# GpSimd's sums in pieces of 256 columns and a new order of all operations, in a causal attention with a squared-ReLU feed-forward behind it

## The chip, the cores and the metric

The kernel runs on one core of a Trainium2 chip. A core has a tensor engine (TensorE, PE in the profile, its weight loads PEld), a vector engine (VectorE, DVE), a scalar engine (ScalarE, ACT), GpSimd (POOL) and a sync engine (SP). Each takes its own instructions in the order of the program and waits by semaphores for the others. Transfers between the chip's memory and the core's are issued by SP, ACT or POOL and carried by 16 DMA engines. The metric is the device time of one execution in microseconds; smaller is better.

## The reference

Eight batches of eight heads, 576 tokens, 16 beacon tokens ahead of the keys, head size 64; then a feed-forward layer over all 4608 tokens. Inputs and outputs are float32.

```python
k_all = np.concatenate([beacon_k, k], axis=2)
v_all = np.concatenate([beacon_v, v], axis=2)
scores = scale * np.matmul(q, k_all.transpose(0, 1, 3, 2))
scores = np.where(causal, -1000000000.0, scores)
a = np.exp(scores - scores.max(-1, keepdims=True))
a /= a.sum(-1, keepdims=True) + 1e-09
x = np.matmul(a, v_all)            # then as (4608, 512)
h = x @ w_in                       # 512 -> 2048
r = np.maximum(h, 0.0)
out = (r * r) @ w_out              # 2048 -> 512
```

## The kernel before

**Attention** works on 32 pairs of heads, four pairs a batch; pair p belongs to batch p // 4. The operations have names. `qk*` are the score products (five visits a batch into PSUM strips), `exp*` the exponentials on ScalarE, `mask*` the causal masks on the diagonal blocks of the probabilities `pt` (DVE by a minimum with the constant `tri`, L780; or GpSimd by a select, L776; five a pair), `av{p}.0.{h}` the products with V of one head (15 matmuls, L802), `norm*` the division by the row sum on DVE (L819, L821). From batch 2 on, q, k and v are loaded by GpSimd's queue (`ld{b}q*`, `ld{b}k*`, `ld{b}v*`; L408, L417, with the beacon rows L416 in part 0), q and k are turned by a DMA transpose on SP (`tr*`), and from batch 3 on the result is turned into `xT` by DMA transposes `xt{b}.{t}` (L853). Batches 0 and 1 are turned by TensorE. Batch 0's first rows come by loads on SP and ACT (`fldk*`, `fldq*`), the rest of it by GpSimd (`sld0k1.*`, `sld0q1.*`, L472).

**Feed-forward** works on nine chunks of 512 tokens. `s1.*` is the first layer, `s2.*` the second. In chunks 3 to 8 the first layer, and in chunks 1 to 8 the second, is done by a scheme of seven products of half size instead of eight: blocks of the inputs, of the weights and of the squared activations are first added or subtracted (`xsum{j}.{n}` L961, `asum*` L928, `wsum*` L913, `sum{j}.{n}.{i}` L1163), and the products' results are put together when they leave PSUM (`h*`, L1023 and L1016; `ev*`, L1217). `s2.{j}.{n}.{t}` is product n of chunk j for token half t, eight matmuls; `s1.{j}.{u}.{n}` product n of unit u, four or eight matmuls. Product 6 of the second layer reads sum 2, product 5 sum 1, product 7 sum 3, product 3 sum 4. `sum{j}.{n}.{i}` covers half i of the eight row blocks: 128 x 1024 elements; each may run on DVE or GpSimd. `relu*` and `sq*` are the activations.

**The order** of all operations is written out by hand in the string `SEQUENCE` (L18 on); a letter behind `@` names the engine where there is a choice (`A` ScalarE, `D` DVE, `P` GpSimd). `Order.run` issues the operations in that order, so the string fixes the queue of each engine, the rotation of PSUM banks and strips, and the order of the loads on each DMA queue. An operation's place in the string is not its time: an engine that is ahead runs its part early. 60 filler matmuls (`fill*`, L354) keep TensorE busy while the first data come. The durations in the calls of `add` are figures that are not used at run time.

Of the kernel before, what the change touches and what calls it, by code (L numbers as in the profile page):

```python
# [12 lines left out]
ALU = mybir.AluOpType  # L13
# [4 lines left out]
ones fill19 fillg19 fill7 fillg7 fill47 fill59 fillg59 fillg47 fill10 fill55 fill34 fillg55 fillg34 fill48 fillg48  # L18
fill23 fillg23 fill45 fillg45 fill43 fill2 fillg2 fill25 fillg25 fillg43 fill35 fill27 fillg27 fillg35 fill33 fill32
fillg33 fillg32 fill57 fillg57 fill58 fill22 fill42 fillg58 fillg22 fillg42 fill40 fill11 fillg11 fillg40 fill56  # L20
fillg10 fill36 fillg36 fillg56 fill46 fillg46 fill39 fill31 fillg31 fldk0 ident fldk1 bkl0 fck1 fck0 bkc0 tp0.0.0k
fillg39 ek0.0.0@D fill29 fillg29 fill9 fillg9 fill49 fillg49 fill21 fillg21 tpg0.0.0k fill28 fill51 fillg51 fillg28
tpb0 fill8 fillg8 ekb0 sld0k1.0 tri fldq0 fldq1 ld0v1 sld0q1.0 ld0v0 fldq2 fcq1 fcq0 tp0.0.0q fill26 fillg26 eq0.0.0@A
fill17 fillg17 tpg0.0.0q tp0.0.1k fill52 fillg52 tp0.0.1q fill38 fillg38 ek0.0.1@D eq0.0.1@A tp0.1.0k tp0.1.1k
ek0.1.0@A ek0.1.1@D fcq2@D tpg0.0.1k tpg0.0.1q tpg0.1.1k fldk2 fck3 fcq3@A qk0.0.0 qk1.0.0 fill41 fillg41 tpg0.1.0k
tp0.0.3q fill6 fill54 fillg6 fillg54 fill18 fillg18 tp0.0.3k fill14 fill5 eq0.0.3@D tpg0.0.3q fillg14 fillg5 tp0.1.0q
tp0.1.1q tp0.0.2q exp0.0.0 exp1.0.0 eq0.1.0@A ek0.0.3@D eq0.0.2@A qk3.0.0 qk0.1.0 mask0.0.0@D eq0.1.1@D fck2
mask1.0.0@D tpg0.0.2q tpg0.1.0q tpg0.0.3k fill13 tpg0.1.1q fillg13 fill4 av0.0.0 fillg4 bkl1 exp3.0.0 fill44 fill12
tp0.0.2k qk1.1.0 fillg12 fillg44 sld0k1.2 sld0q1.2 ld0v3 ld0v2 win0 ld0v4 mask3.0.0@P win2 exp0.1.0 fill0 fill30
norm0.0.0 av1.0.0 ek0.0.2@D fillg30 tpg0.0.2k fillg0 norm1.0.0 exp1.1.0 qk1.1.2 av3.0.0 tp0.1.2k xtp0.0.0 xte0.0.0@D  # L30
norm3.0.0 qk2.0.0 exp1.1.2 exp2.0.0 ek0.1.2@D fill1 tp0.1.2q qk0.1.2 mask2.0.0@D eq0.1.2@D fillg1 fill53 fill37
fillg37 fillg53 tpg0.1.2k qk0.1.1 fill16 fillg16 fill3 fillg3 av2.0.0 fill50 fill24 fillg24 tpg0.1.2q exp0.1.2
exp0.1.1 qk1.1.1 fillg50 win1 mask1.1.1@P norm2.0.0 xtp0.0.3 tp0.1.3k xte0.0.3@D qk2.1.1 ek0.1.3@D exp1.1.1
mask0.1.1@P win3 sld1k0.0 sld1q0.0 sld1k0.2 mask1.1.0@D xtp0.0.2 fill15 fillg15 tpg0.1.3k tp0.1.3q fill20 fillg20
eq0.1.3@D xtp0.0.1 mask0.1.0@D qk2.1.0 bkc1 xte0.0.2@D exp2.1.1 exp2.1.0 mask2.1.0@P ld2q6 av1.1.0 norm1.1.0
mask2.1.1@D qk2.1.2 qk3.1.0 tpg0.1.3q xte0.0.1@A av0.1.0 s1.0.3.0 xtp0.1.1 s1.0.8.0 exp2.1.2 exp3.1.0 wout1 sld1q0.2
ld2q7 ld1v1 ld1v0 wout0 ld2q4 zero2 wout2 ld1v3 qk3.1.1 qk3.1.2 norm0.1.0 relu0.8.0@A tpb1 xte0.1.1@D mask3.1.1@D
# [190 lines left out]
def kernel(  # L228
# [709 lines left out]
    def add_first_both(j, G, sq):  # L938
# [18 lines left out]
        for n, o, a, c in ((1, pieces(s[1]), b12, b11), (2, pieces(s[2]), b22, pieces(s[1])), (3, b12, b22, b12),  # L957
                           (4, pieces(s[4]), b21, pieces(s[2]))):
            def emit_x(e, o=o, a=a, c=c):
                for x, y, z in zip(o, a, c):  # L960
                    (nc.vector if e == "DVE" else nc.gpsimd).tensor_tensor(out=x, in0=y, in1=z, op=ALU.subtract)  # L961
# [381 lines left out]
```

## Time and profile before

| what | before |
|---|---|
| median of 3 runs | 324.85 us (324.58 to 325.82) |
| the profiled execution | 325.59 us, span 323.9 us |
| TensorE busy | 313.9 us, 97% of the span, 3882 matmuls |
| VectorE busy | 252.1 us, 78% |
| ScalarE busy | 213.1 us, 66% |
| GpSimd busy | 195.8 us, 60%, 268 instructions |
| granted TensorE clock | 0.999 |
| sums of L1163 on GpSimd | 19, 2.1 to 2.5 us each |

How to read the rows below: L12 is line 12 of the kernel. Rows of groups give line, engine, operation, out<-in by the program's names, shape and count, then busy us and mean ns of one, then the idle time of that engine just before them and what ended it. Rows of a timeline give start and length in us from the span's start, engine, line, operation and count; in brackets the idle time before and who ended it. A row of the waits reads: who waited, on which line, for whom: us in total, times, longest. Matmuls overlap one another, so a row's length can exceed the spacing of matmuls.

### The profile page before, as it was taken

To read this page: it belongs to the slowest core of one execution; us is meant where nothing else is said; L and a number is where in the kernel's file an instruction comes from. 1 tells how busy PE (TensorE), PEld (TensorE's weight loads), DVE (VectorE), ACT (ScalarE), POOL (GpSimd) and SP (SyncE) were. 2 spreads that over 40 slices of the span, in tenths; PEclk is the share of its full clock that TensorE was granted. 3 is DMA by queue.
4 is the path that set the end of the run, shared out by engine and by line. 5 is a ranking of instruction groups with operands and counts; after the bars stand their busy time and mean duration, and the time that the engine had idled before them with its cause. 6 is when DMAs were issued, how large, how long until landed. Compare 5 with 4: busy or idle time off the path is not lost.

```text
span 323.9 us, 9406 instructions
## 1 busy us (share of the span) xinstructions
PE 313.9 (97%) x3882; PEld 247.4 (76%) x3882; DVE 252.1 (78%) x529; ACT 213.1 (66%) x313; POOL 195.8 (60%) x268
## 2 busy tenths in 40 slices
PE   7899999999999999998999999999999989999995
PEld 5569765644886468887788888888898878888884
DVE  2687698758976798789997998896867987695773
ACT  2785588257677794768657996889767545555720
POOL 8574679496189588888293759956606051535340
PEclk9999999999999999999999999999999999999999
DMA  8999999999999999999799969944523430110043
GB/s 162 178 179 200 189 182 114 146 199 178 146 78 157 198 174 84 124 222 155 61 130 135 212 68 128 149 88 142 49 16 91 110 52 0 68 65 2 0 148 113
DMA packets 153188, 39.60 MB, mean 122 GB/s; under 512 B 140730, under 2 KB 148794, under 8 KB 153146
## 3 DMA queue, kind: packets, MB, share of 16 engines
q0 software_dynamic: 103744, 18.10, 71.7%
q1 hardware_dynamic: 48253, 20.29, 30.3%
q10 hardware_dynamic: 1149, 0.62, 0.7%
q8 instruction: 30, 0.49, 0.6%
q14 instruction: 12, 0.10, 0.1%
HBM read 37.22 MB, written 9.44 MB: 144 GB/s over the span
## 4 chain that ended last, share of the span: by engine, by line
PE 89%; DVE 3%; DMA 3%; ACT 2%; issue 1%; POOL 0%; DVEq 0%; POOLq 0%; ACTq 0%
PE ps L1194 28%; PE ps L985 21%; PE ps L1088 13%; PE ps L802 9%; PE strip L649 6%; PE ps L1137 4%; DMA qk_area<-in_k_dram 3%; PE ps L649 2%; PE strip L1194 2%; DVE g L1023 1%; PE ps L870 1%; PE ps L354 1%; ACT pt L747 1%; PE ps L489 1%; PE ps L487 1%
## 5 line engine op out<-in xcount | busy, mean ns | idle before, releaser
L1194 PEld LDWEIGHTS <-g 128*128 128x128 bf16 x768 | 72.7, 98 | 10.8 <-issue 1.4
L747 ACT ACTIVATE pt<-strip 128x1024 bf16<-128x1024 f32 x70 | 70.2, 1032 | 5.7 <-PE strip L649 5.7
L1023 DVE CUSTOM_DVE_ANT_0 g<-ps,spare 128x512 bf16<-128x512 f32 x72 | 48.8, 686 | 17.9 <-PE ps L985 12.1
L1194 PE MATMUL ps<-w_out,g 128*128 128x256 bf16 x480 | 60.9, 273 | 0.0
L776 POOL TENSOR_SCALAR_AFFINE_SELECT pt<-pt 128x256 bf16<-128x256 bf16 (+1 forms) x80 | 33.3, 437 | 27.9 <-ACT pt L747 23.9
L372 ACT COPY spare<-ps 128x512 f32<-128x512 f32 x54 | 31.5, 588 | 25.9 <-PE ps L985 21.7
L1163 POOL TENSOR_TENSOR g<-g 128x1024 bf16<-128x1024 bf16 x13 | 28.0, 2158 | 31.5 <-DVE g L1163 10.8
L408 POOL DMA_DIRECT2D qk_area<-in_q_dram x48 | 35.2, 742 | 17.3 <-DMA qT<-qk_area 14.3
L985 PEld LDWEIGHTS <-w_in 128*128 128x128 bf16 x480 | 39.3, 96 | 7.6 <-issue 2.7
L1088 PE MATMUL ps<-xT,w_in 128*128 128x512 bf16 (+2 forms) x256 | 44.1, 326 | 0.0
L985 PE MATMUL ps<-xT,w_in 128*128 128x256 bf16 (+4 forms) x384 | 42.7, 247 | 0.3 <-DMA xT<-xn 0.2
L802 PE MATMUL ps<-vb,pt 128*128 128x65 bf16 (+1 forms) x960 | 38.5, 194 | 1.8 <-DVE g L1023 0.9
L802 PEld LDWEIGHTS <-pt 128*128 128x128 bf16 (+1 forms) x960 | 35.6, 97 | 5.9 <-issue 2.6
L417 POOL DMA_DIRECT2D vb<-in_v_dram x40 | 34.4, 860 | 6.2 <-DMA qk_area<-in_q_dram 2.3
L1088 PEld LDWEIGHTS <-w_in 128*128 128x128 bf16 x256 | 24.0, 98 | 16.3 <-issue 1.0
L1049 ACT ACTIVATE g<-g 128x1024 bf16<-128x1024 bf16 x31 | 32.2, 1058 | 5.6 <-DVE g L1023 4.1
L821 DVE TENSOR_TENSOR xn<-ps,rcp 128x320 bf16<-128x320 f32 (+2 forms) x64 | 31.5, 492 | 2.2
L985 PEld LDWEIGHTS <-qk_area 128*128 128x128 bf16 x320 | 27.8, 97 | 5.2 <-issue 0.8
L747 ACT ACTIVATE pt<-ps 128x512 bf16<-128x512 f32 x42 | 23.6, 598 | 9.6 <-PE ps L649 8.8
L1194 PE MATMUL ps<-w_sum,g 128*128 128x256 bf16 x224 | 28.9, 273 | 0.0
L985 PE MATMUL ps<-spare,qk_area 128*128 128x256 bf16 x192 | 27.9, 272 | 0.5 <-DVE spare L961 0.5
L649 PEld LDWEIGHTS <-kT 64*128 64x128 bf16 x618 | 19.8, 94 | 10.7 <-issue 7.8
(87 smaller groups left out, 492.0 us busy)
## 6 DMA issues: line engine op xcount, KB each, us to landing
out_dram<-osb SPq DMA_DIRECT2D x16, 512.0 KB, 3.8
qk_area<-in_q_dram POOLq DMA_DIRECT2D x48, 72.0 KB, 4.8
vb<-in_v_dram POOLq DMA_DIRECT2D x24, 128.0 KB, 6.0
qk_area<-in_k_dram POOLq DMA_DIRECT2D x18, 128.0 KB, 4.7
w_in<-in_moe_w_in_dram POOLq DMA_DIRECT2D x4, 512.0 KB, 9.4
w_out<-in_moe_w_out_dram POOLq DMA_DIRECT2D x4, 512.0 KB, 9.2
vb<-in_v_dram POOLq DMA_DIRECT2D x8, 112.0 KB, 5.2
qk_area<-in_k_dram POOLq DMA_DIRECT2D x6, 112.0 KB, 4.5
```

What stands on the lines that cost most here:

```text
L372: nc.scalar.copy(dst, src)
L408: return [nc.gpsimd.dma_start(out=qb[:, g, :, D * u:D * u + D], in_=t[b, c].rearrange("(n p) d -> p n d", p=NP))]
L417: insts.append(nc.gpsimd.dma_start(out=dst[lo:rows], in_=t[b, :, t0:t0 + rows - lo, :].transpose([1, 0, 2])))
L649: nc.tensor.matmul(out, kc[b % 2][hp, c, pr] if b >= NPE else kT[b % 2][hp, pr, 128 * c:128 * c + 128], rhs, start=True, stop=True)
L747: nc.scalar.activation(out, in_, AF.Exp, bias=0.0, scale=scale)
L776: nc.gpsimd.affine_select(out=d[:, :, i], in_=d[:, :, i], compare_op=ALU.is_ge, fill=0.0, base=Nb if m0 + i == 0 else 0, pattern=[[0, 2], ...
L802: nc.tensor.matmul(a[:, at + (t - tl[0]) * (D + 1):at + (t - tl[0] + 1) * (D + 1)], P[0:rr, hj, o:o + 128], vb[b % 2][0:rr, c, 2 * pr + hj ...
L985: nc.tensor.matmul(o[:, i * HT + at:i * HT + at + w], lhs[:, m, f * 128:(f + 1) * 128], part[:, m], start=fresh and i == 0 and at == 0 and ...
L1023: nc.vector._custom_dve(TENSOR_ADD_SAT, out=dst, in0=bank_of(chain), in1=held[keep[added].held[1]].rearrange("p (f t) -> p f t", f=2), s0= ...
L1049: nc.scalar.activation(both, both, AF.Square, bias=0.0, scale=1.0)
L1088: nc.tensor.matmul(h[:, lo - spans[0][0]:hi - spans[0][0]], w_in_sb[:, mc, ft * 128:(ft + 1) * 128], xT[:, mc, lo % RING:lo % RING + hi - lo],
L1194: nc.tensor.matmul(o, lhs[:, f, t * 128:(t + 1) * 128], rhs[:, f], start=fresh and f == 0, stop=f == HF - 1, skip_group_check=True)
```

## The change

Two helpers change. A sum of the activations (`add_sum`) and a sum of the inputs (`emit_x`) stay one instruction on DVE; on GpSimd a sum becomes four instructions of 256 columns (one per row block), and an input sum one instruction per row block and part of the ring, 256 columns or fewer each, where it was one instruction with both row blocks.

```diff
             def emit_x(e, o=o, a=a, c=c):
                 for x, y, z in zip(o, a, c):
-                    (nc.vector if e == "DVE" else nc.gpsimd).tensor_tensor(out=x, in0=y, in1=z, op=ALU.subtract)
+                    if e == "DVE":
+                        nc.vector.tensor_tensor(out=x, in0=y, in1=z, op=ALU.subtract)
+                        continue
+                    for m in range(HM):
+                        nc.gpsimd.tensor_tensor(out=x[:, m], in0=y[:, m], in1=z[:, m], op=ALU.subtract)
...
         def add_sum(n, o, a, c, op, i, deps):
             fs = slice(4 * i, 4 * i + 4)
-            sums[n].append(add(f"sum{j}.{n}.{i}", ("DVE", "POOL"), {"DVE": 0.67, "POOL": 2.12}, lambda e: (nc.vector if e == "DVE" else nc.gpsimd).tensor_tensor(
-                out=o[:, fs], in0=a[:, fs], in1=c[:, fs], op=op), deps=deps))
+
+            def emit(e):
+                if e == "DVE":
+                    nc.vector.tensor_tensor(out=o[:, fs], in0=a[:, fs], in1=c[:, fs], op=op)
+                    return
+                for f in range(4 * i, 4 * i + 4):
+                    nc.gpsimd.tensor_tensor(out=o[:, f], in0=a[:, f], in1=c[:, f], op=op)
+
+            sums[n].append(add(f"sum{j}.{n}.{i}", ("DVE", "POOL"), {"DVE": 0.67, "POOL": 2.12}, emit, deps=deps))
```

The string `SEQUENCE` is replaced as a whole, with the same 1737 words (other letters on some). Counted over the string: sums on GpSimd 19 before, 17 after (45 and 47 on DVE); input sums on GpSimd 6 and 3; masks on GpSimd 78 and 77; evacuations `ev*` on ScalarE 23 and 28, on DVE, where there is a choice, 17 and 12. From chunk 3 on TensorE's own order is nearly the old one; ahead of it it differs much, as do the other engines' orders throughout. Excerpts that are spoken of below, the loads and masks of GpSimd at the end of batch 4 first:

```diff
-... mask18.0.1.1@P mask19.0.0.0@P mask19.0.0.1@P mask18.0.2@P ld6q4 mask18.0.0.1@P ld6q5 ld6q6 mask18.0.1.0@P ld6q2 ld5v2 qk20.2 av18.0.0 sq3.2.1@D norm18.0.0 s1.3.3.3 h3.3.c12 av19.0.0 av18.0.1 av19.0.1 s2.3.2.0 sq3.3.0@A norm18.0.1 norm19.0.1 sum3.1.0@P ...
+... mask18.0.1.1@P ld5v4 ld6q1 mask18.0.1.0@P mask18.0.2@P ld5v3 ld6q2 mask19.0.0.1@P ld6q0 ld6q6 av18.0.0 s1.3.3.4 h3.3.c21@A sq3.3.1@A qk20.2 av18.0.1 s1.3.3.3 norm18.0.0 mask19.0.2@P mask19.0.0.0@P mask19.0.1.0@P mask19.0.1.1@P ld6k4 ld6q7 av19.0.0 sum3.1.0@D sum3.3.0@P ...
```

The start of chunk 7:

```diff
-... av31.0.1 norm31.0.0 h6.3.c22 h6.3.c21@A sq6.3.1@A sq6.2.0@A av30.0.1 norm31.0.1 norm30.0.1 s1.6.3.3 s1.6.3.2 s2.6.2.0 s2.6.2.1 st11 xt6.3 xt6.4 st10 xt6.2 xt7.0 h6.3.c12 h6.3.c11 sq6.3.0@D sum6.1.1@D xsum7.1@D xsum7.2@D s2.6.1.0 s1.7.0.1 s1.7.1.1 h7.0.c1@A s1.7.0.6 h7.0.u2@A s2.6.1.1 sum6.3.1@D xsum7.3@D xsum7.4@D s1.7.0.7 h7.0.u3@A s1.7.0.4 ...
+... av31.0.1 h6.3.c22 h6.3.c21@A sq6.3.1@A norm31.0.0 s1.6.3.3 s1.6.3.2 norm31.0.1 s2.6.2.0 s2.6.2.1 xt6.3 st11 xt7.0 st10 h6.3.c12 h6.3.c11 sq6.3.0@D sum6.1.1@D xsum7.1@D xsum7.2@D xsum7.3@D sum6.3.1@D xsum7.4@D s1.7.0.1 s2.6.1.0 h7.0.c1@A s1.7.0.6 h7.0.u2@A s2.6.1.1 s1.7.0.7 s1.7.1.1 h7.0.u3@A ev6.c1.None@A s1.7.0.4 ...
```

The first operations of the queues at the start (SP; ACT; GpSimd; before, then after):

```diff
-fldk0 fldk1 bkl0 fldk2; fldq0 fldq1 fldq2 fcq1 fcq0; ident sld0k1.0 tri ld0v1 sld0q1.0 ld0v0
+fldk2 fldk1 bkl0 fldk0; fldq0 fldq1 fldq2 fcq0 fcq1; ident tri sld0k1.0 sld0q1.0 ld0v1 ld0v0
```

GpSimd's queue ahead of `av24.0.0` after the change, from the first mask of pair 25, and the second layer of chunk 7 after it:

```diff
+mask25.0.0.1@P ld7q1 ld7v3 ld7k0 ld7k4 ld7k1 ld7v4 ld7q0 ld7k3 ld6v0 ld7q6 ld7q2 ld7v1 mask24.0.0.0@P
...
+s2.7.1.1 s1.8.0.3 sum7.3.1@D sum7.2.1@D h8.0.c12 s2.7.2.0 s1.8.1.6 h8.1.u2@D s1.8.1.2 s2.7.2.1 h8.1.c11 ev7.c1.None@A ev7.c11.None sq8.0.1@A sum7.1.0@P sum7.3.0@P sum7.2.0@P sum7.4.0@P s1.8.1.7 s1.8.2.1 h8.1.u3@D h8.2.c1@A s2.7.6.0
```

More of the change, by code (lines that the diff above doesn't have):

```diff
@@ L17 @@
 SEQUENCE = """
[L18 to L37, printed above, removed]
@@ L98 @@
-mask18.0.0.1@P ld6q5 ld6q6 mask18.0.1.0@P ld6q2 ld5v2 qk20.2 av18.0.0 sq3.2.1@D norm18.0.0 s1.3.3.3 h3.3.c12 av19.0.0
-av18.0.1 av19.0.1 s2.3.2.0 sq3.3.0@A norm18.0.1 norm19.0.1 sum3.1.0@P s2.3.1.0 sum3.1.1@D s2.3.5.0 s2.3.1.1 norm19.0.0
-sum3.3.1@D exp20.2.0.0.0 exp20.2.1.0.0 sum3.3.0@D sum3.2.0@D sum3.2.1@D xt4.2 xt4.1 xt4.0 ev3.c1.None@A s2.3.5.1
-s2.3.2.1 ld5v3 sum3.4.0@P ld6v0 ld6k3 ld6k0 s2.3.6.0 s2.3.6.1 ev3.u2.None@A ev3.c11.None mask20.0.0.0@D mask20.0.0.1@D
-qk20.5 exp20.5.-1.0.0 exp20.5.0.0.0 exp20.5.-1.1.0 s2.3.7.0 s1.4.0.1 s2.3.7.1 h4.0.c1@A ev3.u3.None@A s1.4.0.2 ld6k4
@@ L163 @@
-sum8.3.0@P h8.3.c12 ev7.c12.None sq8.3.0@A s2.8.1.0 s2.8.1.1 sum8.1.1@D sum8.3.1@D sum8.2.0@D sum8.2.1@D s2.8.5.0
-s2.8.2.1 sum8.4.1@P sum8.4.0@D st14 ev7.c21.None@A ev8.c1.0@A s2.8.6.0 ev8.u2.0@D st15 ev8.c1.1@A ev8.c11.None
-st8.0.0.0 s2.8.5.1 s2.8.7.0 ev8.u3.0@D ev8.c22.0 s2.8.6.1 ev8.u2.1@D s2.8.4.0 ev8.c21.0@D st8.1.0.0 st8.0.1.0 s2.8.7.1
-ev8.u3.1@D ev8.c22.1 s2.8.3.0 s2.8.4.1 s2.8.3.1 ev8.c12.0 st8.0.0.256 ev8.c21.1@A ev8.c12.1 st8.1.1.0 st8.0.1.256
+ones fill23 fillg23 fill54 fill58 fillg58 fillg54 fill12 fill15 fill53 fillg53 fillg15 fill7 fillg7 ident tri fill29
@@ new lines @@
+fillg12 fill57 fill22 fillg22 fill43 fillg43 fillg57 fill33 fillg29 fill16 fill40 fillg40 fillg16 fill13 fillg13 fill6
+fill35 fillg35 fill49 fillg49 fillg6 fill21 fillg21 fillg33 fill2 fill39 fillg39 fldq0 fillg2 fill38 fillg38 fill25
+fill20 fillg20 fill59 fillg59 fillg25 fill34 fill44 fillg34 fill37 fillg37 fill41 fill50 fillg41 fillg44 fill48
+fillg50 fill10 fillg10 fillg48 fldk2 fldk1 bkl0 fill32 fill8 fillg32 fillg8 fck3 bkc0 tpb0 fill9 fillg9 fill26 fillg26
+fldq1 fldk0 fldq2 fck1 ekb0 fck0 tp0.0.1k fill19 fillg19 fill3 fillg3 fill46 fillg46 fill1 fillg1 fill42 fillg42
@@ new lines @@
+exp18.11.1.0.0 h3.2.c1@D s1.3.2.6 norm17.0.0 s1.3.3.2 s1.3.3.6 sq3.0.0@D h3.3.c11 h3.2.c11 h3.2.u2@A qk19.13 s1.3.2.7
+sq3.1.0@A h3.2.u3@A av17.0.1 s1.3.2.5 exp19.13.1.0.0 h3.3.u2@D norm17.0.1 s1.3.2.4 h3.2.c21@A h3.2.c22 sq3.1.1@D
+sq3.2.1@D s1.3.3.7 h3.3.u3@A s1.3.3.5 s1.3.2.3 h3.2.c12 h3.3.c22 exp19.13.0.0.0 ld6q3 ld6q4 ld6q5 mask18.0.1.1@P ld5v4
+ld6q1 mask18.0.1.0@P mask18.0.2@P ld5v3 ld6q2 mask19.0.0.1@P ld6q0 ld6q6 av18.0.0 s1.3.3.4 h3.3.c21@A sq3.3.1@A qk20.2
+av18.0.1 s1.3.3.3 norm18.0.0 mask19.0.2@P mask19.0.0.0@P mask19.0.1.0@P mask19.0.1.1@P ld6k4 ld6q7 av19.0.0 sum3.1.0@D
@@ new lines @@
+sum3.3.0@P h3.3.c12 s2.3.2.0 av19.0.1 sq3.2.0@A s2.3.2.1 norm18.0.1 norm19.0.0 norm19.0.1 xt4.2 xt4.0 xt4.1 sq3.3.0@A
+s2.3.1.0 s2.3.1.1 ev3.c1.None@A exp20.2.1.0.0 exp20.2.0.0.0 sum3.1.1@D sum3.3.1@D sum3.2.1@D sum3.2.0@D s2.3.5.0
+s2.3.5.1 s2.3.6.0 s2.3.6.1 sum3.4.0@D ev3.c11.None qk20.5 ev3.u2.None@A exp20.5.-1.1.0 xsum4.1@D xsum4.2@D
+exp20.5.-1.0.0 exp20.5.1.0.0 mask20.0.1.0@D s2.3.7.0 s1.4.0.1 s2.3.7.1 h4.0.c1@A s1.4.0.2 s1.4.0.6 ev3.u3.None@A
+s2.3.4.0 xsum4.4@D mask20.0.2@D h4.0.c11 ev3.c22.None xsum4.3@D s1.4.0.5 s2.3.4.1 h4.0.u2@A exp20.5.0.0.0 s1.4.0.7
@@ new lines @@
+h5.1.c1@D ev4.u2.None@A s1.5.0.5 s1.5.0.7 s2.4.7.0 s1.5.1.6 mask24.0.0.1@D h5.0.u3@A s1.5.0.4 h5.0.c21@A h5.0.c22
+s1.5.0.3 sum4.4.0@D h5.0.c12 h5.1.u2@A s2.4.7.1 qk25.8 s1.5.1.7 ev4.u3.None@D exp25.8.-1.1.0 exp25.8.-1.0.0 s2.4.4.0
+exp25.8.0.0.0 exp25.8.1.0.0 s1.5.1.2 s2.4.4.1 qk27.13 s1.5.1.5 ev4.c21.None@A s1.5.2.1 exp27.13.0.0.0 ld7k4 ld7k1
+ld7v4 ld7q0 ld7k3 ld6v0 mask24.0.1.0@D ld7q6 ld7q2 sq5.0.1@D h5.1.u3@D sum4.4.1@D ld7v1 h5.1.c11 mask24.0.1.1@D
+mask24.0.0.0@P ld7k2 mask27.0.1.0@P mask25.0.2@P ld7v2 mask25.0.1.1@D mask26.0.0.0@P mask24.0.2@D h5.1.c22 av24.0.0
```

249 lines of the change are left out of this document (129 added, 120 removed).

## The prediction

> **What bounds the kernel now.** I read the page's first part and its chain, then who TensorE waits for, then the stretches in which it waits.
>
> ```profile
> span 323.9 us, 9406 instructions
> PE 313.9 (97%) x3882; PEld 247.4 (76%) x3882; DVE 252.1 (78%) x529; ACT 213.1 (66%) x313; POOL 195.8 (60%) x268
> PE 89%; DVE 3%; DMA 3%; ACT 2%; issue 1%; POOL 0%; DVEq 0%; POOLq 0%; ACTq 0%
> ```
>
> TensorE is 97% busy and carries 89% of the chain that ended last; GpSimd carries 0% of it. The change leaves every matmul as it is, so it can only take away or add waits of TensorE. This is all the waiting there is (us in total, times, longest):
>
> ```profile
> PE ps L354 <- DVE ones L348: 1.8, 1, 1.8
> PE ps L487 <- DMA qk_area<-in_k_dram: 1.2, 1, 1.2
> PE ps L802 <- DVE g L1023: 0.9, 1, 0.9
> PE ps L985 <- ACT spare L372: 0.7, 1, 0.7
> PE ps L802 <- DVE pt L780: 0.5, 1, 0.5
> PE ps L985 <- DVE spare L961: 0.5, 1, 0.5
> PE ps L802 <- DVE xn L821: 0.3, 1, 0.3
> PE ps L985 <- DMA xT<-xn: 0.2, 1, 0.2
> ```
>
> The sum is 6.1 us, of which 3.0 (the first two rows) lie in the start, before there is data. The other 3.1 lie in two places: at 153 to 157 us, where the last two pairs of batch 4 are multiplied with V (L802: 0.9 + 0.5 + 0.3), and at 258 to 263 us, where chunk 7 begins (L985: 0.7 + 0.5 + 0.2). Nothing that touches the second half can gain more than 3.1 us, 1.0% of the span.
>
> **The change, part by part.** The profiled execution took 325.59 us for a span of 323.9, so 1.7 us lie around the span; it is 0.74 above the median of 324.85. All terms below are differences, made on the span of 323.9 and then set on the median.
>
> *1. Four pieces for one sum.* One line groups instructions by form (count, then busy us, mean ns); the timeline rows give start and length, for both instructions where it says x2.
>
> ```profile
> L1163 POOL TENSOR_TENSOR g<-g 128x1024 bf16<-128x1024 bf16 x13 | 28.0, 2158 | 31.5 <-DVE g L1163 10.8 <-PE ps L1194 9.7 <-ACT pt L747 8.8
> 224.09 1.30 POOL L961 TENSOR_TENSOR spare<-xT,spare 128x384 bf16<-128x384 bf16 x2 [1.04 <-DVE spare L961]
> 225.36 1.41 POOL L961 TENSOR_TENSOR xT<-xT 128x384 bf16<-128x384 bf16 x2
> ```
>
> Two stretches of the chain give what one product of the second layer (L1194) and two of the first (L985) take on TensorE, 0.87 and 2 x 0.44 us:
>
> ```profile
> 200.16 0.87 PE ps L1194 x8
> 201.03 0.89 PE ps L985 x8
> ```
>
> No sum in 256-column pieces is in this trace. The nearest are those of L961 that cross the ring's end: 512 columns in two pieces (384 and 128) take 1.30 or 1.41 us, so four pieces of 256 take 2.60 to 2.82 against 2.16 for one instruction: 0.44 to 0.66 more each. Below, pieces that cost nothing extra give 0; a gain is excluded, since the columns are the same. I take 0.44, as those pieces run back to back as the new ones will. The new order gives GpSimd 17 sums instead of 19 and 3 input sums (xsum) instead of 6, so its work grows by 17 x 0.44 = 7.5 us and falls by two sums, 4.3 us, and the xsums. It is 60% busy, and no TensorE wait names it: I put it at 0. Its tightest consumer in the new order is sum 2 of chunk 7 (`sum7.2.0@P`): between `s2.7.1.1`, which it must wait for, and `s2.7.6.0`, which reads it, stand five first-layer products and two of the second (5 x 0.44 + 2 x 0.87 = 3.9 us). 2.60 fits, with 1.3 us to spare; one instruction would have left 1.8.
>
> The Trainium skill, GPSIMD Engine Reference, section 2.1, has the cost of one more instruction as one indirect call, some tens of cycles: three more would then cost, as an estimate from that page, about 0.1 us, not 0.44, and the sum stays 0.
>
> *2. What a long sum holds up.* DVE's mask on L780 normally takes 0.28 us (three take 0.64 in a row at 187.78). Beside GpSimd's sums:
>
> ```profile
> 187.78 0.64 DVE L780 TENSOR_TENSOR pt<-pt,tri 128x256 bf16<-128x256 bf16 x3
> 151.01 2.06 DVE L780 TENSOR_TENSOR pt<-pt,tri 128x256 bf16<-128x256 bf16 x2
> 153.21 2.15 POOL L1163 TENSOR_TENSOR s_sum<-g 128x1024 bf16<-128x1024 bf16 x1
> 153.72 0.61 PE L802 MATMUL ps<-vb,pt 128*128 128x65 bf16 x15 [0.87 <-DVE g L1023]
> 154.19 1.33 DVE L780 TENSOR_TENSOR pt<-pt,tri 128x256 bf16<-128x256 bf16 x1
> 155.58 0.94 PE L802 MATMUL ps<-vb,pt 128*128 128x65 bf16 x25 [0.48 <-DVE pt L780]
> ```
>
> The mask at 154.19 ends 0.16 us after the sum at 153.21 does (155.36): it stood still for about 1.05 us. TensorE's 0.48 at 155.58 and the 0.3 on `xn` behind it come from that; no other wait in the list ends on a mask. A piece of 256 columns would hold a mask for 0.65 at most (2.60 / 4). But the largest wait, 0.87, comes from DVE being stuck at 151.01, before any sum starts: GpSimd runs masks and issues loads there. The split doesn't touch that.
>
> *3. The new order at that place.* `sum3.1.0` goes to DVE, and the masks of pair 19 all go to GpSimd, behind masks of 18 and loads. What lies between the end of pair 18's exponentials and `av19.0.0` on its queue: six 128-row masks, two 80-row masks, four q loads, two v loads.
>
> ```profile
> L776 POOL TENSOR_SCALAR_AFFINE_SELECT pt<-pt 128x256 bf16<-128x256 bf16 x69 | 30.2, 454 | 23.0 <-ACT pt L747 19.2 <-ACT pt L671 3.7
> L776 POOL TENSOR_SCALAR_AFFINE_SELECT pt<-pt 80x160 bf16<-80x160 bf16 x11 | 3.6, 333 | 4.8 <-ACT pt L747 4.7
> L408 POOL DMA_DIRECT2D qk_area<-in_q_dram x48 | 35.2, 742 | 17.3 <-DMA qT<-qk_area 14.3 <-DMA w_out<-in_moe_w_out_dram 1.8 <-PE ps L1088 1.2
> L417 POOL DMA_DIRECT2D vb<-in_v_dram x40 | 34.4, 860 | 6.2 <-DMA qk_area<-in_q_dram 2.3 <-DMA qk_area<-in_k_dram 1.6 <-DMA w_in<-in_moe_w_in_dram 1.5
> 146.90 1.84 POOL L776 TENSOR_SCALAR_AFFINE_SELECT pt<-pt 128x256 bf16<-128x256 bf16 x4 [2.33 <-ACT pt L747]
> ```
>
> 6 x 0.454 + 2 x 0.333 + 4 x 0.742 + 2 x 0.860 = 8.1 us from 146.9, when the exponentials free GpSimd: 155.0. TensorE would reach `av19.0.0` at about 154.4 (without the 0.87 at 153.9, and 0.5 of products now stand ahead of it). So 0.6 of waiting replaces 0.87 + 0.48 + 0.3 = 1.65. Parts 2 and 3 together: -1.0 if the 0.87 goes, near 0 if it stays beside the new 0.6; at best -1.65. I take -0.8.
>
> *4. Chunk 7.* Its first product needs the transposed rows of batch 7, which wait for the last normalised pair.
>
> ```profile
> 255.80 2.39 DMA xT<-xn
> 259.87 0.61 PE L985 MATMUL ps<-spare,qk_area 128*128 128x256 bf16 x4 [0.48 <-DVE spare L961]
> 262.48 0.60 PE L985 MATMUL ps<-spare,w_in 128*128 128x256 bf16 x4 [0.67 <-ACT spare L372]
> ```
>
> The new order has one second-layer product less ahead of `s1.7.0.1` (0.87 of cover lost), but one normalisation less behind the last product with V (before, two stood in a row), and puts that product between `s1.7.0.1` and `s1.7.0.6` and one first-layer product ahead of `s1.7.0.4`, where 0.48 and 0.67 were waited. The wait in front (0.2 now) becomes 0.2 to 1.0, the two behind 0.1 to 0.6: against 0.2 + 0.48 + 0.67 = 1.35 that is -1.0 to +0.3. I take -0.2, since the transfer's 2.39 us stays on the path.
>
> *5. The start.* GpSimd now makes the mask constant `tri` ahead of `sld0k1.0`, the load for which TensorE waits 1.2 us, and SP and ACT issue their first loads in another order (`fldk2` first, `fldk0` last).
>
> ```profile
> 1.58 0.89 POOL L472 DMA_DIRECT2D qk_area<-in_k_dram  x1 [0.20 <-issue]
> ...
> 2.87 0.54 POOL L345 TENSOR_SCALAR_AFFINE_SELECT tri<-tri 128x128 bf16<-128x128 bf16 x2
> ...
> 10.04 0.49 PE L487 MATMUL ps<-ident,qk_area 112*64 112x112 bf16 x12 [1.24 <-DMA qk_area<-in_k_dram]
> ```
>
> The load leaves 0.9 us later: issued by 2.47 now, `tri` done at 3.41. It takes 8.4 us, beside the other first loads; if these bound it, nothing is lost, if its own issue does, all 0.9. On DVE three casts and an evacuation now stand ahead of the first scores. Against that 16 instead of 21 filler matmuls stand behind the first scores, 0.11 us each by two fillers in a row when the clock is up: -0.5. Range -0.5 to +0.9; I take +0.3, nearer to the upper end because the first wait ends with that very load.
>
> *6. Elsewhere.* The order of the whole program changes, and where TensorE now waits for nothing it may wait. The two places above cost 1.65 and 1.35 us: none such gives 0, one 1.5, two 3. Few moves in the last 170 us are larger than one product, so I take +0.3.
>
> Sum: 0 - 0.8 - 0.2 + 0.3 + 0.3 = -0.4 us: 324.85 - 0.4 = **324.4 us**. A difference of 0.5% (1.6 us) is about what a measurement of this kernel tells from no change; this is less.
>
> **The rivals.** *Faster:* the waits of parts 2 to 4 go nearly all (-2.5 of 3.0), the start gives 0 and no new wait comes: 322.4. For it speaks that DVE's long holds go and that three xsums and two sums return to DVE; against it that 0.87 of the 3.0 was no sum's doing and that the transfer of 2.39 us remains.
>
> *Slower:* GpSimd's queue comes late with the loads it carries. In the new order `ld6v0` moves from far ahead to just before its reader `av24.0.0`, behind nine issues that wait for pair 25's mask.
>
> ```profile
> 192.01 1.02 ACT L747 ACTIVATE pt<-strip 128x1024 bf16<-128x1024 f32 x1
> 207.75 0.62 PE L802 MATMUL ps<-vb,pt 128*128 128x65 bf16 x15
> vb<-in_v_dram POOLq DMA_DIRECT2D x8, 112.0 KB, 5.2
> ```
>
> From 193.0: a mask 0.45, two q issues 1.5, seven issues for k, v and the beacon's rows at 0.86, 6.0: 201.0; its own beacon issue 0.86, then 5.2 to landing: 207.1, when 207.75 is needed: 0.7 us of room. If GpSimd comes 2.4 us later than this (its row of q loads in part 3 shows 14.3 us of waiting for transposes), TensorE waits 1.7 here, and part 3's queue, late too, costs 1.5 more: -0.4 + 3.2 gives 327.6. It decides from 0.7 us of lateness on. Against it: GpSimd is 40% idle.
>
> *The pieces don't help, or come late.* If GpSimd doesn't let go between pieces, holds stay as they are and the split is worth 0. The two masks on GpSimd at 206.22 speak against it: DVE's at 206.26 ended within 0.45, before the second did.
>
> ```profile
> 206.22 0.76 POOL L776 TENSOR_SCALAR_AFFINE_SELECT pt<-pt 128x256 bf16<-128x256 bf16 x2 [0.41 <-ACT pt L747]
> 206.26 0.45 DVE L780 TENSOR_TENSOR pt<-pt,tri 80x160 bf16<-80x160 bf16 x1
> 289.59 2.42 POOL L1163 TENSOR_TENSOR g<-s_sum,g 128x1024 bf16<-128x1024 bf16 x1 [5.47 <-ACT osb L372]
> ```
>
> But then DVE can step in before each piece, as it did before the sum at 289.59, which took 0.26 more than 2.16: up to 3 x 0.68 more a sum, 4.6 in all. At `sum7.2.0` (3.9 of room) that costs 0.7, at the last two sums of chunk 8, back to back, about 1: 324.4 + 1.7 = 326.1. The Trainium skill, SBUF — State Buffer, section "Who interferes with whom", states this as a rule: the one that starts first holds the pair of ports for the whole instruction, so more, shorter instructions also mean more openings for the other side.
>
> **How the numbers follow.** Forecast 0.40, faster rival 0.28, late queue 0.22, late pieces 0.10. Predicted 324.4, the forecast's own range 323.0 to 325.9. The range reaches from 321.2 (all of 3.1 and the fillers' 0.5) to 328.0 (the late queue and a little more). Faster by over 0.5% (below 323.2): the rival's 0.28 and 0.03 of the forecast; slower (above 326.5): 0.22, and 0.04 of the late pieces; the rest, 0.43, within.
>
> **What would show it.** In the profile of the changed kernel: four POOL rows of L1163 a sum, 0.55 to 0.7 us each; no DVE mask or sum over 1.0 us beside one of them; the L802 waits at 153 to 157 below 1.0 in total, the first of them ended by GpSimd's masks; the waits at chunk 7's start about 1.1; the first L487 matmul of the second part at 10.3 to 10.9. I am wrong if a TensorE wait of over 1 us stands at a place not named here, or if one ends on GpSimd's sums.

## The result, and the profile after

| kernel | median us | ratio to the kernel before, 95% interval | lowest us |
|---|---|---|---|
| before (8 runs beside the changed one) | 325.48 | | 324.33 |
| changed kernel (8 runs) | 323.10 | 0.9931 [0.9910, 0.9952] | 322.73 |
| the same again (12 runs, later; 35 runs of the kernel before beside it, median 325.36) | 323.16 | 0.9928 [0.9902, 0.9954] | 322.70 |

The change makes the kernel about 2.3 us faster (325.48 x 0.0069 = 2.2; 325.36 x 0.0072 = 2.3). The ratios leave out three runs over 1.5% above the fastest of their kernel: one of the kernel before (329.13) and two of the kernel with `tri` behind the loads below (328.37 and 328.29). The profiled execution took 323.34 us. The page's first part, the chain's shares and all waits of TensorE in it:

```profile
span 321.6 us, 9484 instructions
PE 314.5 (98%) x3882; PEld 247.3 (77%) x3882; DVE 249.6 (78%) x526; ACT 217.1 (68%) x324; POOL 196.9 (61%) x316
PE 91%; DVE 5%; issue 1%; ACT 1%; DMA 1%; POOL 0%; DVEq 0%; ACTq 0%; POOLq 0%
PE ps L355 <- DVE ones L349: 1.8, 1, 1.8
PE ps L990 <- DVE g L1056: 0.7, 1, 0.7
PE ps L990 <- DVE g L1028: 0.4, 1, 0.4
PE ps L990 <- ACT spare L373: 0.2, 1, 0.2
```

The waits fall from 6.1 to 3.1 us and the span by 2.3. The three L802 rows of the place at 153 to 157 us (0.9 + 0.5 + 0.3; the line is L803 now) are gone, and so is the 1.2 us for the first load. At the start of chunk 7 (L990, L985 before) 0.68 and 0.22 us are left, 0.9 instead of 1.4, as the two rows behind this paragraph show. The 0.4 on L990 lies elsewhere, at 185.85, where the list of before has nothing. No row names GpSimd. Of the 3.0 us less of waiting 0.7 does not reach the span: TensorE's busy time is 0.6 longer for the same 3882 matmuls (314.5 against 313.9); why is not known.

```profile
256.07 0.61 PE L990 MATMUL ps<-xT,w_in 128*128 128x256 bf16 x4 [0.68 <-DVE g L1056]
260.25 0.60 PE L990 MATMUL ps<-spare,w_in 128*128 128x256 bf16 x4 [0.22 <-ACT spare L373]
```

The place at 152 to 164 us in the timeline, GpSimd and then TensorE, and the largest group of pieces:

```profile
152.41 1.77 POOL L777 TENSOR_SCALAR_AFFINE_SELECT pt<-pt 80x160 bf16<-80x160 bf16 x4
155.60 2.55 POOL L1174 TENSOR_TENSOR g<-g 128x256 bf16<-128x256 bf16 x4
160.37 3.32 POOL L1174 TENSOR_TENSOR g<-g 128x256 bf16<-128x256 bf16 x4 [2.22 <-DVE g L1171]
154.63 0.62 PE L803 MATMUL ps<-vb,pt 128*128 128x65 bf16 x15
L1174 POOL TENSOR_TENSOR g<-g 128x256 bf16<-128x256 bf16 x44 | 29.6, 708 | 18.4 <-DVE g L1171 12.6 <-PE ps L1206 5.0 <-DVE s_sum L1171 0.8
```

GpSimd's last masks of pair 19 end at 154.18, before `av19.0.0` starts at 154.63. A sum in four pieces takes 2.55 us when it is left alone and 3.32 when DVE steps in between two pieces; a piece's mean of 0.71 holds such waits.

### The profile page after: what moved, and what is told of

Same layout as the page of the kernel before. It is cut to its first block, busy times and chain, and to the rows that moved or that the text cites. A ratio compares the mean times of both kernels' runs of the same rounds, so it can differ in the third digit from the quotient of the medians.

```text
span 321.6 us, 9484 instructions
## 1 busy us (share of the span) xinstructions
PE 314.5 (98%) x3882; PEld 247.3 (77%) x3882; DVE 249.6 (78%) x526; ACT 217.1 (68%) x324; POOL 196.9 (61%) x316
## 4 chain that ended last, share of the span: by engine, by line
PE 91%; DVE 5%; issue 1%; ACT 1%; DMA 1%; POOL 0%; DVEq 0%; ACTq 0%; POOLq 0%
PE ps L1206 28%; PE ps L990 21%; PE ps L1093 13%; PE ps L803 8%; PE strip L650 7%; PE ps L1142 4%; PE ps L355 3%; PE ps L650 2%; PE strip L1206 2%; DVE g L1028 2%; DVE xn L822 1%; PE ps L871 1%; PE ps L488 1%; PE ps L490 1%; DMA xT<-xn 1%
## 5 line engine op out<-in xcount | busy, mean ns | idle before, releaser
L777 POOL TENSOR_SCALAR_AFFINE_SELECT pt<-pt 128x256 bf16<-128x256 bf16 (+1 forms) x78 | 31.9, 429 | 45.1 <-ACT pt L748 41.6
L1093 PE MATMUL ps<-xT,w_in 128*128 128x512 bf16 (+2 forms) x256 | 45.2, 326 | 0.0
L990 PEld LDWEIGHTS <-w_in 128*128 128x128 bf16 x480 | 39.4, 96 | 7.0 <-issue 2.5
L990 PE MATMUL ps<-xT,w_in 128*128 128x256 bf16 (+4 forms) x384 | 41.8, 247 | 0.7 <-DVE g L1056 0.7
L1174 POOL TENSOR_TENSOR g<-g 128x256 bf16<-128x256 bf16 x44 | 29.6, 708 | 18.4 <-DVE g L1171 12.6
L803 PE MATMUL ps<-vb,pt 128*128 128x65 bf16 (+1 forms) x960 | 38.2, 193 | 0.1
L803 PEld LDWEIGHTS <-pt 128*128 128x128 bf16 (+1 forms) x960 | 35.5, 97 | 3.3 <-issue 0.6
L1054 ACT ACTIVATE g<-g 128x1024 bf16<-128x1024 bf16 x30 | 31.1, 1067 | 2.3 <-DVE g L1028 1.5
L990 PEld LDWEIGHTS <-qk_area 128*128 128x128 bf16 x320 | 27.5, 97 | 5.5 <-issue 1.7
L418 POOL DMA_DIRECT2D qk_area<-in_k_dram x30 | 25.4, 850 | 4.2 <-DMA kT<-qk_area 1.8
```

The lines of the kernel that those rows point to most:

```text
L418: insts.append(nc.gpsimd.dma_start(out=dst[lo:rows], in_=t[b, :, t0:t0 + rows - lo, :].transpose([1, 0, 2])))
L777: nc.gpsimd.affine_select(out=d[:, :, i], in_=d[:, :, i], compare_op=ALU.is_ge, fill=0.0, base=Nb if m0 + i == 0 else 0, pattern=[[0, 2], ...
L803: nc.tensor.matmul(a[:, at + (t - tl[0]) * (D + 1):at + (t - tl[0] + 1) * (D + 1)], P[0:rr, hj, o:o + 128], vb[b % 2][0:rr, c, 2 * pr + hj ...
L990: nc.tensor.matmul(o[:, i * HT + at:i * HT + at + w], lhs[:, m, f * 128:(f + 1) * 128], part[:, m], start=fresh and i == 0 and at == 0 and ...
L1093: nc.tensor.matmul(h[:, lo - spans[0][0]:hi - spans[0][0]], w_in_sb[:, mc, ft * 128:(ft + 1) * 128], xT[:, mc, lo % RING:lo % RING + hi - lo],
```

## The experiments

After the result two theories stood against each other. *Place:* the new order made the gain, by taking the masks off DVE at 151 us and `sum3.1.0` off GpSimd. *Pieces:* the split made it. The first four kernels take the two apart.

**Split alone, order alone.**

The first, against the kernel before, takes over the two helpers as the diff above shows them and keeps the order; the second, against the changed kernel, takes them back and keeps the new order:

```diff
-                for f in range(4 * i, 4 * i + 4):
-                    nc.gpsimd.tensor_tensor(out=o[:, f], in0=a[:, f], in1=c[:, f], op=op)
+                nc.gpsimd.tensor_tensor(out=o[:, fs], in0=a[:, fs], in1=c[:, fs], op=op)
```

> The order before with the sums in pieces. If the new order makes the gain (place theory): DVE's mask at 151.01 still takes 2 us, since no sum runs there, and the 0.87 us wait of av18.0.0 stays; only the 0.48 + 0.3 behind the mask at 154.19 can go, so -0.8 to 0 us, a ratio of 0.9975 to 1.000 to the kernel before. If the split makes it (piece theory): both waits go and the ratio is 0.992 to 0.995, like the changed kernel's 0.9931. If the pieces cost something on the path: above 1.000.

> The new order with each of GpSimd's sums as one instruction again. Place theory: the waits at 150 to 157 us stay gone, since no sum of GpSimd runs there before av19.0.0, and the ratio is 0.992 to 0.995; DVE holds of 1 to 2 us come back beside the 17 sums, but most of them behind TensorE's back, 0 to +0.5 us. Piece theory: most of the gain goes, ratio 0.998 to 1.000, and TensorE waits for a DVE operation that stands beside a sum.

The split alone: 323.31 us, ratio 0.9927 [0.9898, 0.9956]. The order alone: 326.73 us, 1.0024 [1.0001, 1.0046]. The place theory falls: the split has the whole gain, and the new order without it is if anything slower than the old one. The timeline of the order alone, at the two sums beside which it loses:

```profile
161.04 2.44 POOL L1163 TENSOR_TENSOR g<-g 128x1024 bf16<-128x1024 bf16 x1 [3.30 <-DVE g L1163]
161.54 2.50 DVE L1163 TENSOR_TENSOR g<-g 128x1024 bf16<-128x1024 bf16 x1
164.69 0.34 PE L649 MATMUL ps<-qT,kT 64*128 64x224 bf16 x4 [0.82 <-DVE osb L1217]
287.38 2.28 POOL L1163 TENSOR_TENSOR g<-s_sum,g 128x1024 bf16<-128x1024 bf16 x1 [8.01 <-PE ps L1194]
287.78 2.43 DVE L1163 TENSOR_TENSOR g<-s_sum,g 128x1024 bf16<-128x1024 bf16 x1
290.87 0.61 PE L985 MATMUL ps<-xT,w_in 128*128 128x256 bf16 x4 [1.43 <-DVE g L1023]
```

A DVE sum that takes 0.68 us alone takes 2.50 and 2.43 beside GpSimd's, and both end 0.6 us after GpSimd's sum does. Behind it on DVE stands an evacuation, and TensorE waits for that: 0.82 + 1.43 = 2.25 us. The second pair is `sum7.2.0` and `sum7.2.1`. TensorE's waits in this trace add up to 3.4 us more than in the changed kernel's; 0.84 of that is a gap at 157.50 for which the profile names no cause, and it is not placed.

**That one sum on DVE, or the masks on GpSimd.**

```diff
-... sum3.1.0@P ...
+... sum3.1.0@D ...
```

```diff
-... s1.3.3.4 mask19.0.1.1@D mask19.0.2@D h3.2.c12 exp19.13.0.0.0 h3.2.c21@A h3.3.c22 mask19.0.1.0@D ... ld6q2 ld5v2 qk20.2 ...
+... s1.3.3.4 h3.2.c12 exp19.13.0.0.0 h3.2.c21@A h3.3.c22 ... ld6q2 ld5v2 mask19.0.1.1@P mask19.0.2@P mask19.0.1.0@P qk20.2 ...
```

> The kernel before with sum3.1.0 alone on DVE, so that no sum of GpSimd stands beside the mask at 154.19. Place theory, first part: that mask takes 0.28 to 0.4 us, the 0.48 in front of av19.0.0 and the 0.3 behind it go, the 0.87 in front of av18.0.0 stays: -0.5 to -0.8 us, ratio 0.9975 to 0.9985. If the sum's 0.67 us on DVE delays the norms or the evacuations there: 0.999 to 1.001. If sums make all of the loss, the 0.87 goes too: 0.995.

> The kernel before with the last three masks of pair 19 on GpSimd, behind its loads, as the new order has them, and sum3.1.0 still one instruction on GpSimd. Place theory: DVE isn't stuck at 151.01 any more, h3.2.c12 comes 1.5 us earlier, the 0.87 goes; GpSimd ends the masks at about 154.7, so up to 0.5 of waiting in front of av19.0.0: -0.9 to -1.7 us, ratio 0.995 to 0.997. If the transfers issued by GpSimd, not the masks' engine, hold whatever DVE runs there, h3.2.c12 or the squares are held instead, and the ratio is 0.999 to 1.001.

One sum moved: 323.48 us, 0.9939 [0.9913, 0.9964], as much as the whole change within the intervals, where the place theory gave at most 0.8 us. The masks moved: 327.35 us, 1.0023 [0.9993, 1.0053], no gain. Its timeline says why:

```profile
154.36 1.05 POOL L776 TENSOR_SCALAR_AFFINE_SELECT pt<-pt 128x256 bf16<-128x256 bf16 x3
155.37 2.12 POOL L1163 TENSOR_TENSOR s_sum<-g 128x1024 bf16<-128x1024 bf16 x1
153.84 4.21 DVE L1051 TENSOR_TENSOR g<-g 128x1024 bf16<-128x1024 bf16 x1
158.74 0.61 PE L802 MATMUL ps<-vb,pt 128*128 128x65 bf16 x15 [2.32 <-DVE xn L821]
```

The masks stand right in front of the sum there. DVE's square (`sq3.2.1`, 0.68 us alone) stood still for 3.5 us, over an issue, three masks and the sum, and did not get in between them. This profile is of the longest of the 12 runs (325.16 to 329.14). Soon after the wait of 2.32 us the granted TensorE clock was 0.5 for 3.4 us, and 16 products of L1194 took 3.54 us where 16 take 1.91 at 166.24: 1.6 us more that are no wait.

**The kernel before once more, and one sum in pieces.** The first four left a question: in the first profile of the kernel before, the largest wait there came from a mask stuck at 151.01, beside no sum. The split could not have removed that.

In the one kernel nothing is changed; the other has the order before and pieces for `sum3.1.0` alone, every other sum and the input sums whole (the branch issues one instruction):

```diff
-                if e == "DVE":
+                if e == "DVE" or f"{j}.{n}.{i}" not in ("3.1.0",):
```

> The kernel before, unchanged, looked at once more. If DVE's 2 us at 151 in the first profile belong to the kernel: a hold of over 1.5 us at 151 to 153 again, beside no sum. If two instructions that start within 0.05 us of one another decide it, and the other kernels with the same order there show none: the masks take 0.43 us for both, the square behind them stands still beside sum3.1.0 instead, for 1.5 to 2.5 us, and TensorE waits for a normalisation in front of av19.0.1. The wait at 10 us may be anything from 0 to 1.3 us, as in the three kernels with the same start.

> The order before, all of GpSimd's sums whole but sum3.1.0, which comes in four pieces. If that one sum costs the order before its loss (one-sum theory, from the run with it on DVE): as much gain as with all sums in pieces, -1.2 to -2.4 us, ratio 0.9925 to 0.9965. If the holds beside all the sums add up: a third or less of it, ratio 0.998 to 1.000.

The kernel before again, one execution (329.09 us, span 327.4; of the 105 other runs of this kernel one took longer):

```profile
155.56 0.91 POOL L417 DMA_DIRECT2D vb<-in_v_dram  x1
156.48 2.14 POOL L1163 TENSOR_TENSOR s_sum<-g 128x1024 bf16<-128x1024 bf16 x1
154.19 0.43 DVE L780 TENSOR_TENSOR pt<-pt,tri 128x256 bf16<-128x256 bf16 x2
155.85 2.92 DVE L780 TENSOR_TENSOR pt<-pt,tri 128x256 bf16<-128x256 bf16 x1
158.83 0.94 PE L802 MATMUL ps<-vb,pt 128*128 128x65 bf16 x25 [1.62 <-DVE pt L780]
PE ps L487 <- DMA qk_area<-in_k_dram: 2.0, 1, 2.0
PE ps L985 <- DMA xT<-xn: 1.6, 2, 1.4
```

The two masks that held the first profile up (2.06 us together) take 0.43 here. The third one, beside `sum3.1.0`, stands still instead: 2.92 us for 0.28. I had expected the square; it was the mask ahead of it. TensorE loses 1.62 (and 0.3 behind it, on `xn`), more than the 0.87 + 0.48 + 0.3 of the first profile. So here the sum was the cause, and the stuck masks at 151.01 belonged to the first execution: in the five other profiles with these masks on DVE the two take 0.43 us, or 1.03 in one (the kernel with one sum in pieces). That the sum is the usual cause rests on the runs with it on DVE and in pieces, not on this one execution. (The last two rows, waits for transfers, are taken up below.)

The one sum in pieces: 324.20 us, 0.9965 [0.9934, 0.9997]; lowest 322.77, the same as with all sums in pieces. That is the edge of the one-sum range; its 12 runs scatter up to 327.2. Its timeline has no wait at the place:

```profile
152.47 3.21 POOL L1169 TENSOR_TENSOR s_sum<-g 128x256 bf16<-128x256 bf16 x4
152.39 0.28 DVE L780 TENSOR_TENSOR pt<-pt,tri 128x256 bf16<-128x256 bf16 x1
152.59 0.68 DVE L1051 TENSOR_TENSOR g<-g 128x1024 bf16<-128x1024 bf16 x1
152.98 1.58 PE L802 MATMUL ps<-vb,pt 128*128 128x65 bf16 x45
```

All 45 matmuls with V run in one row; it is GpSimd that waits now (3.21 instead of 2.55).

**Both edits, and two sums in the new order.** The first kernel joins the split with `sum3.1.0@D`; the second is the new order with whole sums and pieces for 3.4.1 and 7.2.0 alone.

> The order before with all sums in pieces and sum3.1.0 on DVE. With the pieces alone DVE's square at 152.02 was still held for 1.58 us and TensorE waited 0.85 us for the normalisation behind it. If that wait is what the pieces leave: -0.4 to -0.9 us against the pieces alone, ratio 0.989 to 0.992, faster than the changed kernel. If the loss was that one sum and nothing else, so that either edit takes all of it: the same as each alone, 0.9925 to 0.995.

> The new order with whole sums but two, sum3.4.1 and sum7.2.0, beside which the order alone showed DVE held for 1.81 and 1.74 us and TensorE waiting 0.82 and 1.43 us. If these two holds are what the order loses without the split: nearly the time of the changed kernel, ratio 0.993 to 0.996. If the other 15 sums and the input sums cost as well: 0.998 to 1.002.

Both edits: 323.84 us, 0.9946 [0.9917, 0.9975]; lowest 322.69. No further gain: within the intervals either edit takes the whole loss. The pieces can still leave a wait there, as in the profile of the split alone:

```profile
151.50 0.91 POOL L417 DMA_DIRECT2D vb<-in_v_dram  x1
152.42 3.01 POOL L1173 TENSOR_TENSOR s_sum<-g 128x256 bf16<-128x256 bf16 x4
152.02 2.26 DVE L1055 TENSOR_TENSOR g<-g 128x1024 bf16<-128x1024 bf16 x1
154.97 0.61 PE L802 MATMUL ps<-vb,pt 128*128 128x65 bf16 x15 [0.85 <-DVE xn L821]
```

The square stood still for 1.6 us here, over the rest of an issue and past the gap behind the first piece.

Two sums split in the new order: 323.91 us, 0.9967 [0.9944, 0.9989], lowest 323.58. Between none in pieces (1.0024) and all (0.9928) lie 0.0096, 3.1 us; two of 17 bring back 0.0057, 1.9 us. That is 60%, just short of the range; by the medians (326.73, 323.91, 323.16) it is 2.8 of 3.6 us, near 80%, and each interval is 0.7 us wide to either side, so the share is only rough. Part of the rest is visible: a mask held 0.5 us beside a whole input sum, behind it an evacuation and 0.25 of waiting at 139.41, and 0.7 of waiting for a transposed `kT`.

**Two pieces instead of four; the start; chunk 7.** All three change the changed kernel, which ran again beside them.

```diff
-                for f in range(4 * i, 4 * i + 4):
-                    nc.gpsimd.tensor_tensor(out=o[:, f], in0=a[:, f], in1=c[:, f], op=op)
+                for f in range(4 * i, 4 * i + 4, 2):
+                    nc.gpsimd.tensor_tensor(out=o[:, f:f + 2], in0=a[:, f:f + 2], in1=c[:, f:f + 2], op=op)
```

```diff
-ident tri sld0k1.0 sld0q1.0
+ident sld0k1.0 sld0q1.0 tri
```

```diff
-s1.7.0.1 s2.6.1.0 h7.0.c1@A s1.7.0.6 h7.0.u2@A s2.6.1.1 s1.7.0.7
+s2.6.1.0 s1.7.0.1 h7.0.c1@A s2.6.1.1 s1.7.0.6 h7.0.u2@A s1.7.0.7
```

> The changed kernel once more, beside the other three on one chip, for its spread. The kernels in the order before, with that sum in pieces or on DVE, reach the changed kernel's lowest time (322.7 to 322.9) but scatter by 2 to 4 us, with waits for transfers of 0.7 to 2.1 us that come in one execution and not in another. If the new order takes the places where such waits come: 322.6 to 323.6 in all runs, ratio 0.991 to 0.995. If its first eight runs were close together by chance: single runs of 324 to 326 as well.

> The new order with each of GpSimd's sums in two pieces of 512 columns instead of four of 256. If a DVE operation stands still until the piece before it ends: holds of up to 1.2 us where four pieces gave up to 0.5, a sum of 2.25 to 2.35 us instead of 2.55; TensorE's room at the two costly places (0.82 and 1.43 us lost to holds of 1.8) leaves +0.2 to +1.0 us. If what matters is only that there is a gap at all: no difference to the changed kernel within 0.3 us.

> The changed kernel with the mask constant made behind the first two of GpSimd's loads again. If the load's issue 0.6 us later costs the start something: -0.2 to -0.6 us. If TensorE doesn't wait for that load any more (no wait on it in the changed kernel's profile): within 0.2 us of the changed kernel.

> The changed kernel with two second-layer products of chunk 6 moved into the waits at chunk 7's start: s2.6.1.0 ahead of s1.7.0.1, s2.6.1.1 ahead of s1.7.0.6. The first can start when the square on DVE ends, 255.5, and covers the 0.68 + 0.17 us until the transposed rows land; the second covers the time until the input sum. If these waits can be filled: s1.7.0.4 at 259.5 to 260.0 instead of 260.25, -0.3 to -0.8 us. If the chain from the rows over the input sums to s1.7.0.4 sets the end there: the waits move to s1.7.0.7 and s1.7.0.4, -0.2 to +0.3 us.

*Two pieces:* 324.21 us, 0.9954 [0.9931, 0.9977]; 1.05 slower than the changed kernel beside it (323.16). At `sum7.2.0` DVE stands still 0.78 us and TensorE waits 0.46 for it; with four pieces the same sum of DVE takes 0.97 and nobody waits. The rest of the 1.05 I have not placed.

```profile
285.48 3.09 POOL L1173 TENSOR_TENSOR g<-s_sum,g 128x512 bf16<-128x512 bf16 x2 [7.64 <-PE ps L1205]
286.10 1.46 DVE L1170 TENSOR_TENSOR g<-s_sum,g 128x1024 bf16<-128x1024 bf16 x1
288.21 0.61 PE L989 MATMUL ps<-xT,w_in 128*128 128x256 bf16 x4 [0.46 <-DVE g L1027]
```

*`tri` behind the loads:* 323.68 us, 0.9944 [0.9919, 0.9970]: 0.5 slower, where I had expected nothing or a gain. GpSimd's load goes out at 1.58 instead of 2.21. The first loads of SP then land later, 5.5 us after their issue instead of 5.1: DVE's cast of one of them starts at 9.12 instead of 8.27, and TensorE waits 0.81 for it. That these loads compete with GpSimd's is argued from the landing times. First that kernel, then the changed one (DVE's rows, and the loads' median times to landing in the first 10 us):

```profile
9.12 0.29 DVE L374 CAST qk_area<-osb 120x256 bf16<-120x256 f32 x1 [1.22 <-DMA osb<-in_k_dram]
9.47 0.28 PE L487 MATMUL ps<-ident,qk_area 120*128 120x120 bf16 x2 [0.81 <-DVE qk_area L374]
qk_area<-in_k_dram POOLq DMA_DIRECT2D x2, 168.0 KB, 7.1
osb<-in_k_dram SPq DMA_DIRECT2D x2, 120.0 KB, 5.5
```

```profile
8.27 0.45 DVE L375 CAST qk_area<-osb 120x256 bf16<-120x256 f32 x1
qk_area<-in_k_dram POOLq DMA_DIRECT2D x2, 168.0 KB, 6.5
osb<-in_k_dram SPq DMA_DIRECT2D x2, 120.0 KB, 5.1
```

*Chunk 7:* 323.12 us, 0.9929 [0.9903, 0.9954], as the changed kernel. The wait of 0.68 in front of `s1.7.0.1` goes, and `s1.7.0.7` waits 0.67 for ScalarE's copy instead; `s1.7.0.4` starts at 260.31 against 260.25. So a chain that these products are not on sets that place, as the second expectation had it; which of its links, the transposed rows, the input sums or ScalarE's copies, was not taken apart. No kernel was faster than the changed one by more than the noise.

*The changed kernel again:* 11 of 12 runs lie at 322.7 to 323.8, one at 324.98, so "all runs" was too much. Over both its series 1 of 20 runs is above 324 us, median 323.15. In the old order with that sum mended (the kernels with the split, with `sum3.1.0@D`, with one sum in pieces, and with both) 20 of 46 are, median 323.84, with the same lowest time (322.69 against 322.70). These series ran on several chips; on the one of the second series the kernel before went from 323.98 to 329.13. The profiles show what comes and goes in the old order: waits for the first load of 0.3 to 2.0 us (four of seven profiles), 1.4 to 1.5 for `xT` (two), 2.1 for `kT` (one). In the six profiles of the new order with `tri` ahead the first two never come; the third does, once, with 0.7.

## Why the prediction was right and wrong

The time (323.1) lies in the range, between the forecast (324.4) and the faster rival (322.4), and below 323.2, which had been given 0.31. That it came within 1.3 us of the forecast is luck in part, two errors against one another: the base is 0.6 higher (325.48 in more runs, not 324.85), and the change brought -2.3, not -0.4. From the first profile of before to that of after the waits change by -1.65 (parts 2 and 3), -0.5 (part 4), -1.2 (part 5) and +0.35 (part 6), -3.0 in all, and 0.7 is lost again in TensorE's longer busy time, which no part had.

- *Parts 2 and 3, the wrong step.* "The largest wait, 0.87, comes from DVE being stuck at 151.01, before any sum starts ... The split doesn't touch that", so -0.8. All 1.65 went, and the split alone, or that sum on DVE alone, gains as much as the whole change. The reading of the row was right for that execution and wrong for the kernel: in the second execution `sum3.1.0` causes 1.62 + 0.3 by itself. The term was -1.65 to -1.9.
- *Part 3's new wait of 0.6 us* did not come: GpSimd began its masks there 0.5 us earlier (146.38) and ended them at 154.18, not 155.0.
- *Part 1* held: 2.60 forecast, 2.55 measured, no TensorE wait on GpSimd. "A piece would hold a mask for 0.65 at most" held for DVE's sums and squares in the changed kernel (at most 0.5), but not with the split alone: a square, 1.6.
- *Part 4*, -0.2: the waits fell by 0.5, from 1.4 to 0.9, inside its range of -1.0 to +0.3. The transfer stayed on the path (2.42 us in the chain after), as it said, and filling the waits gained nothing.
- *Part 5*, +0.3: wrong in sign. The load left 0.6 us later (2.21), not 0.9, and nothing was lost by it. The mask constant ahead of the load is worth about -0.5, and the wait of 1.2 for that load is gone.
- *Part 6*, +0.3 for new waits: with the pieces the changed kernel has one, of 0.35. Without them two places cost 0.82 and 1.43, so the two halves of the change cannot be costed apart: the new order puts whole sums where they hurt, and the pieces make that harmless.
- *The faster rival's* picture (waits of parts 2 to 4 go, no new one) was the nearest, though 0.9 of chunk 7's 1.4 stayed and the start, which it put at 0, gave 1.2 in these profiles. *Late queue:* no wait on `av24.0.0`. *Late pieces:* DVE does step in, and `sum7.2.0` took 3.5 us (3.49 in the second series), 0.9 more than 2.60 and inside the 1.3 of room; no wait.
- *The signs:* a piece takes 0.67 us in the middle (0.55 to 0.7 forecast), and no wait of TensorE ends on a sum of GpSimd or exceeds 1 us behind the start. "No DVE mask or sum over 1.0 us" was just missed: a sum beside pieces took 1.04 (at 160.86), an input sum 1.13 (at 163.11).

Shown by runs: one sum of GpSimd costs the old order 2.0 us by the run with it on DVE (0.9939) and 1.1 by the run with it in pieces (0.9965), most or all of the 2.3; two cost the new order 60 to 80% of what it lacks without pieces. Only argued: that the waits for transfers are rarer in the new order because of its start and its order of loads; of that, only `tri` was tried alone.

## What to carry to other kernels

Cost a long GpSimd instruction by the DVE instructions that can stand beside it and by who waits for what is queued behind those, not by its own length; one such pair may be nearly the whole loss, and here splitting the sum and moving it to DVE were worth the same within the intervals. Before a wait in one profile is put down to a cause that the change doesn't touch, look at a second execution, and at the granted clock in both. An order and the size of its instructions are to be tried crosswise, since each can hide what the other costs.

## What the runs showed of the hardware that was not expected

A hold of DVE is not bounded by one GpSimd instruction: 3.5 us over an issue, three masks and a sum, and 2.6 beside an issue and a sum of 2.14. The Trainium skill, SBUF — State Buffer, section "Who interferes with whom", gives the shared ports to whoever starts first for its whole instruction; the holds beside one sum agree (DVE's sum at 161.54 ends 0.56 us after GpSimd's), and who gets in between several instructions in a row doesn't follow from it. Issues of loads don't always do it: with both edits DVE's mask and square ran beside two of them without delay, as these rows show. What decides between the two is open.

```profile
152.18 1.80 POOL L417 DMA_DIRECT2D vb<-in_v_dram  x2
152.48 0.28 DVE L780 TENSOR_TENSOR pt<-pt,tri 128x256 bf16<-128x256 bf16 x1
152.68 0.68 DVE L1055 TENSOR_TENSOR g<-g 128x1024 bf16<-128x1024 bf16 x1
```

And a load that was issued 0.6 us later did not cost that: with `tri` ahead GpSimd's loads land in 6.5 instead of 7.1 us, and SP's come earlier as well.

A wait of TensorE of over 2 us can cost more than itself. With the masks moved, the granted clock is 0.5 from 159.4 to 162.8 us, soon after the wait of 2.32 us ended at 158.74; in the second execution of the kernel before it is 0.5 from 11.5 to 14.9, soon after the wait of 2.05 ended at 10.45. Behind the wait of 2.13 with `sum3.1.0@D` it stays at 1.0, so what decides is not shown. Such 3.4 us at half speed in a span of 327 us make a mean clock of 0.995: 17 of the 97 runs of the kernel before that have a clock on record lie at 0.990 to 0.995, all at 326.4 us or more, and none of the changed kernel's 20. So part of the old order's scatter is lost clock, not waiting alone.
